# New hand-recorded operation lists, with later planned landings of the first loads, in a fused attention and channel-mix kernel

## The chip, the cores and the metric

The kernel runs on one core of one Trainium2 chip. A core has TensorE (PE, matrix products and transposes into PSUM), VectorE (DVE), ScalarE (ACT), GpSimd (POOL, used here to issue loads) and SyncE (SP, which issues other transfers). The metric is the device time of one execution in microseconds (us). The kernel before was run three times: 231.55, 230.36 and 232.74 us; its time is their median, 231.55 us.

## The reference

Attention over 8 batches, 8 heads, 576 rows of 64 numbers, with a causal window of 128 and a linear penalty for distance, and behind it a channel mix of the RWKV kind on its result:

```python
def _attn_ref(q, k, v):
    scores = np.matmul(q, k.transpose(0, 1, 3, 2)) / np.sqrt(D)
    rel = pos[:, None] - pos[None, :]
    slopes = 2.0 ** (-8.0 * (np.arange(H) + 1) / H)
    mask = (rel >= 0) & (rel < 128)
    scores = np.where(mask, scores - slopes * np.abs(rel), -1e9)
    attn = softmax(scores)
    return np.matmul(attn, v)

def _moe_ref(x, mu_k, mu_r, w_k, w_v, w_r):   # x: [8, 576, 512]
    x_prev = x shifted down by one row, zeros in front
    xk = mu_k * x + (1.0 - mu_k) * x_prev
    xr = mu_r * x + (1.0 - mu_r) * x_prev
    k = np.maximum(xk @ w_k, 0.0)             # 512 -> 1024
    v = k * k @ w_v                           # 1024 -> 512
    r = 1.0 / (1.0 + np.exp(-(xr @ w_r)))     # 512 -> 512
    return r * v
```

q, k, v, the weights and the output are float32 in memory; the products run in bf16.

## The kernel before, in words

**What one group does.** A batch's 8 heads are worked two at a time, in 4 groups (g = 0 to 3). For a group, q and k are brought into transposed form: by PE transposes and copies on ACT or DVE (L696, `copy_any`) in batches 0 to 4, and by transposing DMAs that SP issues (`flip`, L534; eight for a batch) in batches 5 to 7. Then `scores` (L698) multiplies k by q (L726) for the 576 x (128 + 128) band, ACT takes the exp from PSUM into the tile `at` (L740), and DVE multiplies it by a table of penalties (L753; batch 0 adds the penalty on PE instead). `attend` (L759) multiplies `at` by v, with a column of ones in v that gives the row sums (L781), and DVE takes the reciprocal and scales (L793) into `xu`. `xu` is transposed into `xt`: by PE and a copy, or, in batches 6 and 7, by a DMA that SP issues (`out_flip`, L899). `shift` (L863) takes the difference of neighbouring rows (L880) and two mixes, xk and xr (L887), all on DVE.

**The channel mix.** `channel_mix` (L968) is called for chunks of 256 to 512 rows of a pair of batches: eight products with w_k (L983), each followed by a relu on ACT (L990) and a square on DVE or ACT (L964), and then for each 128 rows one product with w_r (L1001), a tanh on ACT (L1008), two half products with w_v (L1017), a DVE step that joins them (L1022), and the store of 128 rows.

**Where the first data come from.** Batch 0 is worked in two parts, rows 0 to 255 and 256 to 575. The first part's q and k come in as float32 by four loads on SP's queue (q) and four on ACT's (k) (`first_load`, L544). All other loads are issued by POOL in program order: `LOADS = 'v2KtVkabRWwc'` gives the order for the beginning: two loads of v, the second part's q and k, the first half of w_k, the tail rows of q and k, two more loads of v and their tail (`tv_load`, L504), the second half of w_k, batch 1's q and k, its tail rows, w_r, the two halves of w_v, batch 1's v. After eight loads POOL waits for the load eight places back.

**What sets the order.** Every piece of work is a node of `Plan` (L89 to 238). A node has an engine, a duration, a latency, the nodes it depends on and the buffers it takes and gives back; `run` (L162) plays the whole kernel through in modelled time, on the host, and emits the instructions in that order. On PE, ACT and DVE the order is not chosen: `ORDER` (L22) lists, for each, the numbers of the operations in the order in which they stand on that engine, and an operation whose number may stand in either of two lists (a copy or a square) goes to the engine that lists it. Operations are numbered as they are added. POOL's order is the program's. SP's order is open: among the transfers that are ready in modelled time the plan takes the one of lowest priority, so that the modelled landing times and durations order SP's stores, flips and out flips. The model of a load is `dma` (L420): its issue, a shared queue named FAB that passes its kilobytes at `RATE`, and a latency of two parts, before and behind. None of these numbers reaches the chip, except through the order.

**Numbers that the prediction uses.** Operations 39 to 128 are the 90 fillers: products of a tile of zeros (L687, `emit_warm`), all depending on nothing but a memset. Operation 131 is the first transpose of q and k, the first real work on PE. Operations 15 to 18 are the DVE memsets of the two `tv` tiles (L480, `late`), for which the first `tv_load` waits. Operation 278 is the first product with w_r, in the place 141 of PE's list. Operations 1028 to 1060 are batch 7's groups 1 to 3; 1033, 1044 and 1055 are their attends. Operation 1090 is the w_r product of the third 128 rows of the chunk that begins at row 512 of the last pair.

Of the kernel before, what the change touches and what calls it, by code (L numbers as in the profile page):

```python
# [52 lines left out]
""".split()],  # L53
    "DVE": [int(x) for x in """
# [16 lines left out]
""".split()],  # L71
}

# [168 lines left out]
def kernel(  # L242
# [12 lines left out]
    nc = tc.nc  # L255
# [235 lines left out]
    def issue_t(nd):  # L491
        return 0.53 + 0.00034 * nd
# [835 lines left out]
```

## Time and profile before

| | |
|---|---|
| median of three runs | 231.55 us |
| the profiled execution: its own time | 230.37 us |
| the profiled execution: span of the core in the trace | 228.6 us |
| mean granted TensorE clock | 0.998 |
| transfers | 32.14 MB in 125629 packets |
| POOL's queue (q0) | 95728 packets, 16.26 MB |
| SP's and ACT's queue (q1) | 28128 packets, 14.89 MB |

The profile is of one execution, recorded on the chip. Times in it count from the start of the span; the execution's own time is 1.8 us longer. A line such as `L983 PE MATMUL uno<-xk,wk_sb ... x416` groups the instructions of line 983: what they write, what they read, how many there are. PEld is the weight load of TensorE, which runs beside the products. "SPq" and "POOLq" are the queues of transfers that SP and POOL issue. In rows with three numbers separated by strokes these are the least, the median and the greatest duration in ns. An arrow in square brackets names what ended an instruction's wait, after the microseconds of the wait. The window table gives for each stretch of the span each engine's busy time and number of instructions, the granted clock of TensorE, the share of the 16 DMA engines' time (a sum over queues, so it can pass 1) and the rate of transfer.

### The profile page before, as it was taken

What the parts mean: (1) busy time and instruction counts of PE and PEld (TensorE: products, weight loads), DVE (VectorE), ACT (ScalarE), POOL (GpSimd) and SP (SyncE); (2) the same over time, 40 slices, a digit from 0 to 9 for tenths busy, and PEclk for the clock granted to TensorE, in tenths of its full rate; (3) what the DMA queues carried; (4) which work ended last, traced back from release to release, by engine and by line L of the source; (5) the groups of instructions that cost most, each with busy time, mean ns of one, the idle gap of its engine ahead of it and who ended that gap; (6) DMA issues with size and microseconds to landing.
All of it is one profiled execution on the core that took longest, in us unless ns stands there. A gap on an engine that the chain in (4) does not pass through costs nothing.

```text
span 228.6 us, 6539 instructions
## 1 busy us (share of the span) xinstructions
PE 223.1 (98%) x2651; PEld 134.3 (59%) x2651; DVE 187.4 (82%) x417; ACT 160.9 (70%) x293; POOL 92.5 (40%) x118
## 2 busy tenths in 40 slices
PE   8999999999999999999999999999999999999994
PEld 8475856665666656545555755545665454456542
DVE  7585999899859999997869997999999986873423
ACT  3679999899998969997576757965758425326511
POOL 8676734889975980965004961600000000000000
PEclk9999999999999999999999999999999999999999
DMA  6999999999999999999965999995162134131123
GB/s 165 179 178 196 196 197 157 194 180 159 197 140 172 129 173 192 150 121 156 232 145 110 179 170 157 119 168 168 46 90 75 49 138 86 46 106 36 46 92 138
DMA packets 125629, 32.14 MB, mean 141 GB/s; under 512 B 112280, under 2 KB 121760, under 8 KB 125600
## 3 DMA queue, kind: packets, MB, share of 16 engines
q0 software_dynamic: 95728, 16.26, 102.5%
q1 hardware_dynamic: 28128, 14.89, 29.9%
q10 hardware_dynamic: 1744, 0.59, 1.1%
q8 instruction: 20, 0.33, 0.6%
q14 instruction: 9, 0.07, 0.1%
HBM read 33.56 MB, written 9.44 MB: 188 GB/s over the span
## 4 chain that ended last, share of the span: by engine, by line
PE 92%; ACT 3%; DMA 3%; SPq 1%; issue 0%; DVE 0%; DVEq 0%
PE uno L1017 28%; PE uno L983 27%; PE uno L1001 14%; PE duo L726 7%; PE duo L781 7%; DMA qx<-in_q_dram 3%; PE uno L837 2%; PE uno L687 2%; PE uno L1078 1%; PE uno L781 1%; PE duo L713 1%; ACT at L740 1%; SPq L550 1%; ACT qk L696 1%; ACT rl L990 1%; PE uno L1123 0%
## 5 line engine op out<-in xcount | busy, mean ns | idle before, releaser
L740 ACT ACTIVATE at<-duo 128x1024 bf16<-128x1024 f32 (+2 forms) x68 | 65.2, 986 | 9.6 <-PE duo L726 9.3
L983 PE MATMUL uno<-xk,wk_sb 128*128 128x256 bf16 (+2 forms) x416 | 71.4, 314 | 0.0
L1017 PE MATMUL uno<-wv_sb,kk 128*128 128x512 bf16 (+2 forms) x296 | 69.0, 374 | 0.0
L990 ACT ACTIVATE rl<-uno 128x256 bf16<-128x256 f32 (+2 forms) x104 | 46.8, 476 | 30.6 <-PE uno L983 25.0
L983 PEld LDWEIGHTS <-wk_sb 128*128 128x128 bf16 x416 | 38.5, 98 | 22.6 <-issue 0.5
L1017 PEld LDWEIGHTS <-kk 128*128 128x128 bf16 x296 | 27.3, 98 | 28.7 <-issue 0.2
L500 POOL DMA_DIRECT2D vs<-in_v_dram x32 | 28.5, 902 | 32.2 <-PE duo L781 29.9
L753 DVE TENSOR_TENSOR at<-at,mask 128x1024 bf16<-128x1024 bf16 x56 | 37.1, 684 | 4.2 <-ACT at L740 4.2
L1001 PE MATMUL uno<-wr_sb,xr 128*128 128x512 bf16 x144 | 36.5, 379 | 0.5 <-ACT rl L990 0.5
L964 DVE TENSOR_TENSOR kk<-rl 128x256 bf16<-128x256 bf16 (+2 forms) x90 | 28.5, 337 | 10.2 <-ACT rl L990 9.9
L1008 ACT ACTIVATE rs<-uno 128x512 bf16<-128x512 f32 x36 | 21.8, 607 | 16.3 <-PE uno L1001 15.2
L1022 DVE SCALAR_TENSOR_TENSOR ot<-rs,uno 128x512 f32<-128x512 bf16 (+2 forms) x37 | 24.4, 667 | 9.4 <-PE uno L1017 6.8
L887 DVE SCALAR_TENSOR_TENSOR xr<-dl,mu_sb,xt 128x576 bf16<-128x576 bf16 (+1 forms) x32 | 24.8, 774 | 0.0
L887 DVE SCALAR_TENSOR_TENSOR xk<-dl,mu_sb,xt 128x576 bf16<-128x576 bf16 (+1 forms) x32 | 24.5, 779 | 0.2
L781 PEld LDWEIGHTS <-at 128*128 128x128 bf16 x576 | 20.8, 98 | 4.2 <-DVE at L753 0.3
L793 DVE TENSOR_TENSOR xu<-duo,rc 128x640 bf16<-128x640 f32 x28 | 22.5, 814 | 0.3
L1001 PEld LDWEIGHTS <-xr 128*128 128x128 bf16 x144 | 13.3, 98 | 13.7 <-DMA wr_sb<-in_moe_w_r_dram 0.6
L531 POOL DMA_DIRECT2D cb<-in_k_dram x20 | 17.8, 910 | 5.6 <-DMA vs<-in_v_dram 4.8
L696 ACT COPY qk<-uno 128x512 bf16<-128x512 bf16 (+1 forms) x33 | 17.4, 588 | 1.8 <-PE uno L1126 1.0
L781 PE MATMUL duo<-vs,at 128*128 128x65 bf16 x448 | 18.6, 194 | 0.0
L531 POOL DMA_DIRECT2D cb<-in_q_dram x20 | 17.7, 924 | 1.0 <-PE duo L781 0.6
L696 ACT COPY xt<-uno 128x512 bf16<-128x512 bf16 (+3 forms) x28 | 15.4, 590 | 1.4 <-PE uno L837 0.7
(83 smaller groups left out, 202.2 us busy)
## 6 DMA issues: line engine op xcount, KB each, us to landing
out_dram<-ot SPq DMA_DIRECT2D x30, 256.0 KB, 4.6
vs<-in_v_dram POOLq DMA_DIRECT2D x32, 128.0 KB, 7.4
cb<-in_q_dram POOLq DMA_DIRECT2D x20, 128.0 KB, 6.7
cb<-in_k_dram POOLq DMA_DIRECT2D x20, 128.0 KB, 6.1
out_dram<-ot SPq DMA_DIRECT2D x10, 128.0 KB, 1.9
wk_sb<-in_moe_w_k_dram POOLq DMA_DIRECT2D x2, 512.0 KB, 8.2
cb<-in_q_dram POOLq DMA_DIRECT2D x4, 256.0 KB, 8.5
cb<-in_k_dram POOLq DMA_DIRECT2D x4, 256.0 KB, 8.8
```

The source lines that it names most:

```text
L500: return dma(POOL, 256, issue_t(1024), lambda e: nc.gpsimd.dma_start(out=vs_buf[h.idx][:, j, :, 0:D], in_=v[b, :, 128 * j:128 * j + 128].r ...
L531: return [dma(POOL, 256, issue_t(1024), lambda e, r=r: nc.gpsimd.dma_start(out=cb_buf[h.idx][:, i, r], in_=src[:, :, r]), [g], kind="q") f ...
L696: (nc.scalar.copy if e == ACT else nc.vector.tensor_copy)(out=out, in_=in_)
L740: lambda e, ah=ah, w=w, hp=hp: nc.scalar.activation(out=ah(), in_=two(hp)[:, :, 0:w], func=AF.Exp, scale=float(scale)), (), [hp])
L753: nc.vector.tensor_tensor(out=a, in0=a, in1=m, op=ALU.mult)
L781: nc.tensor.matmul(a[:, hl, t - t0], lhsT=at[:, lo:lo + 128], rhs=vs[:, u, 2 * g + hl, :] if u < NF else tvb[:, 2 * g + hl], start=(u == u ...
L887: lambda e: nc.vector.scalar_tensor_tensor(out=buf[hk.idx][:, g, e0 + c0:e0 + c1], in0=dls(), scalar=mu[:, g:g + 1], in1=xc(1), op0=ALU.mu ...
L964: nc.vector.tensor_tensor(out=out, in0=in_, in1=in_, op=ALU.mult)
L983: nc.tensor.matmul(one(hp)[:, 0:n], lhsT=wk_sb[:, po, 128 * fo:128 * fo + 128], rhs=xk_buf[hx.idx][:, po, c0:c1], start=(po == 0), stop=(p ...
L990: a = op(ACT, act_t(n), [s], pr, lambda e, hp=hp, hr=hr: nc.scalar.activation(out=rl_buf[hr.idx][:, 0:n], in_=one(hp)[:, 0:n], func=AF.Rel ...
L1001: nc.tensor.matmul(one(hp), lhsT=xr_buf[hx.idx][:, po, 128 * c:128 * c + 128], rhs=wr_sb[:, po], start=(po == 0), stop=(po == NPO - 1))
L1017: nc.tensor.matmul(one(hv)[:, a:b], lhsT=kk_buf[hk.idx][:, fo, o:o + 128], rhs=wv_sb[:, fo, a:b], start=(fo == 0), stop=(fo == NFO - 1))
```

## The change

The three lists in `ORDER` are replaced by others. They hold the same operations; 12 of them change the engine. PE's new list has 26 fillers instead of 31 ahead of operation 131. The four `tv` memsets (15 to 18) stand earlier in DVE's list, ahead of operation 149, batch 0's first reciprocal. Operation 1055 stands ahead of 1044 and 1033 instead of behind them, and 1090 at place 388 instead of 408 (counted from 1).

The plan gets three new constants. `FIRST` adds to the planned latency of the third and fourth of the first q and k loads on each queue, `VFIRST` to the planned kilobytes and latency of batch 0's v loads, `VLATE` 0.9 us to the planned latency of batch 1's. They change no transfer; through `run` they change the order of SP's queue, which is played anew with the new lists. Line numbers behind the constants move down by 3 to 8 lines, in `scores` and all that follows by 8.

The diff, with the inner lines of the lists cut:

```diff
 ORDER = {
     "PE": [int(x) for x in """
-42 76 47 65 59 73 39 58 48 50 71 68 63 74 75 41 43 55 46 61 40 66 51 52 45 56 57 67 70 53 69 131 60 44 49 72 144
-133 146 166 155 93 79 125 97 110 168 54 148 135 157 170 78 151 84 92 127 96 108 37 115 95 99 82 87 105 120 121
-86 106 173 159 64 83 124 118 62 123 81 184 119 128 122 111 138 100 116 90 112 102 85 101 77 98 117 103 162 89
-104 199 91 126 107 88 94 113 114 109 80 187 229 214 202 181 217 232 257 189 204 219 191 206 234 221 260 263 194
...
-904 885 1039 898 887 882 888 916 1028 924 921 892 922 883 926 893 927 1044 1033 976 988 973 1055 982 991 979 985
-1002 994 1007 997 1012 999 1009 1004 1000 1005 1010 1112 1121 1118 1061 1014 1067 1064 1076 1124 1103 1082 1109
-1115 1073 1100 1015 1070 1085 1079 1090 1092 1106 1093 1087 1097 1088 1126 1098 1095 1131 1127 1129 1132 1134
+75 65 44 77 46 42 61 50 41 40 43 59 45 63 53 66 48 57 56 39 72 49 47 76 68 69 131 71 51 67 58 74 144 133 146 52
+55 166 155 62 107 78 79 73 168 148 157 60 106 135 93 111 170 91 124 151 70 120 86 54 109 127 85 98 159 122 128
+101 117 138 87 112 82 84 173 115 108 96 105 121 37 116 81 64 119 123 184 83 114 162 118 100 92 103 102 89 113
+110 104 99 88 80 90 97 126 95 94 125 199 229 187 214 181 202 232 217 189 257 204 191 219 206 234 221 194 260 236
...
+910 901 924 1039 882 887 883 913 888 1028 885 976 973 921 1055 922 994 1044 991 979 926 892 927 1033 982 893 988
+1002 1007 985 997 1004 1012 999 1009 1000 1010 1090 1067 1100 1082 1005 1106 1061 1070 1076 1014 1079 1109 1085
+1115 1103 1064 1073 1015 1087 1124 1118 1088 1095 1097 1092 1121 1112 1098 1126 1093 1127 1131 1129 1132 1134
 1135
 """.split()],
     "ACT": [int(x) for x in """
-10 11 12 13 14 132 145 134 167 147 169 158 152 174 186 139 251 248 200 163 247 188 230 215 203 246 218 233 245
-190 258 205 220 250 259 235 244 261 249 195 264 225 267 255 210 357 270 240 356 256 268 273 325 276 361 359 279
-284 328 330 318 298 341 307 339 289 299 370 372 290 292 301 308 304 463 462 293 473 474 348 347 295 305 296 310
-505 504 313 311 302 378 379 476 478 493 494 509 393 507 399 402 394 496 408 498 396 411 405 406 390 387 421 388
...
-784 848 943 787 963 965 792 954 952 802 869 857 920 872 1020 881 1018 866 908 891 875 863 896 911 878 914 1053
-1051 860 902 886 1040 1042 899 905 917 1029 925 1031 977 989 974 992 983 980 986 1003 995 1008 1013 998 1113
-1062 1119 1122 1068 1077 1065 1125 1104 1083 1116 1074 1110 1071 1086 1080 1091 1101 1107 1096 1130 1137
+10 11 12 13 14 132 145 134 147 167 156 169 158 152 139 174 185 163 250 244 246 230 200 201 248 188 251 203 233
+218 190 247 205 249 220 258 245 235 195 261 210 264 225 267 270 240 357 255 356 256 276 273 325 361 359 279 367
+284 328 330 318 301 339 341 277 370 292 372 302 289 290 298 293 307 473 474 462 463 304 348 347 295 505 296 504
+313 310 305 311 379 308 378 478 476 494 493 507 408 509 399 393 496 498 411 387 402 388 396 390 570 571 421 572
...
+943 848 787 963 965 802 954 857 869 872 952 920 891 1018 1020 863 896 881 878 899 866 875 908 1053 905 860 1051
+902 925 1042 1040 917 914 911 886 977 1031 974 1029 995 980 992 983 1003 989 1008 986 998 1013 1091 1083 1101
+1068 1062 1071 1077 1107 1080 1110 1086 1104 1065 1074 1125 1116 1096 1119 1122 1113 1130 1137
 """.split()],
     "DVE": [int(x) for x in """
-0 2 6 4 7 5 1 34 29 3 28 26 9 27 32 25 30 129 130 31 142 143 15 17 36 8 33 22 35 19 18 156 20 149 136 150 137
-171 172 38 24 16 160 153 161 175 185 176 140 141 201 178 23 154 21 231 216 164 179 165 183 182 180 177 192 193
-207 208 222 223 262 237 238 265 226 196 227 197 228 323 198 326 241 211 243 212 242 368 213 367 336 337 277 271
-329 252 360 253 274 342 331 340 362 371 282 373 344 333 345 334 287 375 376 364 365 352 349 354 460 350 353 351
...
-1046 990 1056 978 1057 975 981 993 984 1058 1060 884 1047 996 1059 987 1048 1036 1037 1001 1038 1006 1011 1049
-1114 1063 1120 1069 1066 1078 1105 1084 1075 1111 1016 1072 1123 1081 1108 1102 1094 1117 1089 1099 1128 1133
-1136
+4 5 6 0 3 9 1 31 36 34 29 2 35 32 30 33 28 25 130 129 27 26 143 142 20 7 19 17 24 15 18 8 16 22 149 150 136 171
+137 172 160 153 161 140 38 175 176 186 178 231 180 21 216 215 182 183 23 141 164 154 165 179 177 192 193 207 208
+222 223 196 237 259 238 262 198 226 268 265 227 323 197 228 326 241 211 242 212 243 213 368 337 336 252 271 253
+329 274 360 331 340 362 342 371 282 287 344 373 345 333 334 375 299 376 364 365 349 352 350 460 353 354 351 383
...
+972 1046 981 1034 928 1035 996 993 894 1058 1059 1047 984 1048 990 1060 987 889 1036 1038 1037 1049 1001 1011
+1006 1102 1069 1084 1063 1078 1108 1111 1081 1105 1066 1072 1016 1075 1120 1089 1117 1123 1114 1094 1128 1099
+1133 1136
 """.split()],
 }
 
@@ -293,6 +293,9 @@
     NO = 5
     WAIT = 0.0
     START, BACK = 1.7, 0.25
+    FIRST = {'SP': (0.0, 0.0, 0.0, 0.7, 1.05, 1.05), 'ACT': (0.0, 0.0, 0.0, 0.85, 1.15, 1.15)}
+    VFIRST = ((0.0, 0.3), (0.0, 0.3), (60.0, 0.5), (60.0, 0.6), (40.0, 0.5))
+    VLATE = {1: 0.9}
     SKEW = {'v': 0.25, 'tv': 0.3, 'ts': 0.3}
     COST = {'first': 0.9, 'v': 1.2, 'q': 0.944, 'ts': 0.66, 'tv': 0.66, 'w': 0.88, 'run4': 1.0, 'run2': 1.03, 'flip': 1.0, 'mu': 1.0, 'x': 1.0}
     SS = ()
@@ -497,14 +500,16 @@
             out=dst()[:, i, h0:h1].rearrange("p h r d -> p h (r d)"), in_=hs), deps, kind='run%d' % r)
 
     def v_load(b, j, h, deps=()):
-        return dma(POOL, 256, issue_t(1024), lambda e: nc.gpsimd.dma_start(
+        return dma(POOL, 256 + (VFIRST[j][0] if b == 0 else 0.0), issue_t(1024), lambda e: nc.gpsimd.dma_start(
             out=vs_buf[h.idx][:, j, :, 0:D],
-            in_=v[b, :, 128 * j:128 * j + 128].rearrange("h p d -> p h d")), deps, kind="v")
+            in_=v[b, :, 128 * j:128 * j + 128].rearrange("h p d -> p h d")), deps, lat=(1.0, 0.9 + (VFIRST[j][1] if b == 0 else VLATE.get(b, 0.0))),
+            kind="v")
 
     def tv_load(b, h, deps=()):
-        return dma(POOL, 128 * TCOST, issue_t(512), lambda e: nc.gpsimd.dma_start(
+        return dma(POOL, 128 * TCOST + (VFIRST[4][0] if b == 0 else 0.0), issue_t(512), lambda e: nc.gpsimd.dma_start(
             out=tv_buf[h.idx][0:64, :, 0:D],
-            in_=v[b, :, SM:S].rearrange("h p d -> p h d")), deps, kind="tv")
+            in_=v[b, :, SM:S].rearrange("h p d -> p h d")), deps, lat=(1.0, 0.9 + (VFIRST[4][1] if b == 0 else VLATE.get(b, 0.0))),
+            kind="tv")
 
     def tail_load(b):
         h = Hold("ts")
@@ -541,13 +546,16 @@
         return dma(POOL, kb, 0.85, lambda e: nc.gpsimd.dma_start(
             out=dst, in_=src.rearrange("(i p) w -> p i w", p=128)), kind="w")
 
+    firsts = {SPE: [], ACT: []}
+
     def first_load(i, g, n):
         hs = (q, k)[i][0, 2 * g:2 * g + 2 * n]
         eng = KQ if i and g < 2 + KLAST else SPE
         qe = nc.scalar if eng == ACT else nc.sync
 
         def put(kb, dst, src):
-            return dma(eng, kb, 0.46, lambda e: qe.dma_start(out=dst, in_=src), lat=(1.54, 0.7), kind="first")
+            firsts[eng].append(kb)
+            return dma(eng, kb, 0.46, lambda e: qe.dma_start(out=dst, in_=src), lat=(1.54, 0.7 + FIRST[eng][len(firsts[eng])]), kind="first")
 
         if g not in FT:
             st = stage[:, g:g + n].rearrange("p g i w -> p (g i w)").rearrange(
```

42 rows, old and new, of the table ORDER are left out of this document.

## The prediction

> **What bounds the kernel now.** I read the page first (busy shares), then the table of windows, then the waits and the timeline around the one place where TensorE (PE) idles, then the tiles of the loads, then the chain of waits.
>
> ```profile
> PE 223.1 (98%) x2651; PEld 134.3 (59%) x2651; DVE 187.4 (82%) x417; ACT 160.9 (70%) x293; POOL 92.5 (40%) x118
> ```
> ```profile
> core 0: us, PE busy (x) PEld busy (x) DVE busy (x) ACT busy (x) POOL busy (x), PEclk, DMA share, GB/s
> 8.90:15.70 6.80, 6.80 (x136) 5.37 (x134) 5.21 (x21) 5.16 (x12) 3.63 (x5) 1.00 1.71 186
> 15.70:24.00 8.30, 8.13 (x149) 4.90 (x147) 5.36 (x18) 7.53 (x17) 5.61 (x9) 1.00 1.55 189
> 24.00:30.60 6.60, 6.10 (x132) 5.03 (x130) 5.79 (x17) 6.41 (x20) 3.88 (x5) 1.00 1.41 200
> 30.60:60.00 29.40, 29.39 (x492) 18.03 (x493) 28.08 (x54) 28.28 (x52) 22.22 (x27) 1.00 2.04 180
> 60.00:100.00 40.00, 40.00 (x585) 24.52 (x584) 36.48 (x74) 37.00 (x68) 28.80 (x35) 1.00 2.03 156
> 100.00:150.00 50.00, 50.00 (x551) 29.00 (x549) 43.42 (x90) 35.96 (x59) 20.77 (x25) 1.00 1.85 157
> 150.00:200.00 50.00, 50.00 (x410) 27.45 (x408) 45.40 (x91) 27.68 (x47) 0.00 (x0) 1.00 0.44 95
> 200.00:222.00 22.00, 22.00 (x128) 12.34 (x126) 9.93 (x24) 8.32 (x20) 0.00 (x0) 1.00 0.21 73
> ```
> The first column is the window, the second its length, the third PE's busy time. From 30.6 to 222 us PE is busy for 191.39 of 191.40 us at a granted clock of 1.00. The change keeps every operation, so after 30.6 us only small things can be won, and a new wait can be lost. What could be won lies before: PE idles 0.17 + 0.50 us between 15.7 and 30.6, and it runs fillers, matmuls on zeros.
>
> ```profile
> L687 PE MATMUL uno<-warm x90: 218/219/314, 1.0 to 15.6; 128*128 128x128 bf16 x90
> ```
> ```profile
> 29.51 0.56 PE L726 MATMUL duo<-qk 64*128 64x256 bf16 x8
> 29.94 0.19 PE L726 MATMUL duo<-tt 64*128 64x64 bf16 x2
> 30.61 1.04 PE L1001 MATMUL uno<-wr_sb,xr 128*128 128x512 bf16 x4 [0.48 <-ACT rl L990]
> ```
> ```profile
> L541 POOL DMA_DIRECT2D wr_sb<-in_moe_w_r_dram x1: 768/768/768, 19.4 to 19.4; - x1
>   PEld L1001: 0.6, 1
> DMA to landing us min/median/max: 11.2/11.2/11.2
> ```
> The last real work before 30.6 is the scores group at 29.51, over by about 30.1; then the first w_r product (L1001) starts at 30.61. Its load was issued at 19.4 and landed 11.2 us later, at 30.6: the weight w_r gates PE there, with some 0.5 us of idle time in front.
>
> **The change, part by part.** The POOL program holds the same transfers in the same order in both kernels. PE's list holds the same 423 operations. Its first 140 places hold the same set in both lists, and place 141 is the same w_r product. So whatever is reordered in front, PE meets the same gate with the same work done.
>
> *Is the gate moved?* One POOL wait should vanish:
>
> ```profile
> 12.71 0.69 POOL L505 DMA_DIRECT2D tv<-in_v_dram  x1 [2.94 <-DVE tv L480]
> 15.13 0.74 POOL L496 DMA_DIRECT2D cb<-in_k_dram  x1 [0.23 <-DMA wk_sb<-in_moe_w_k_dram]
> 18.73 0.68 POOL L521 DMA_DIRECT2D ts<-in_k_dram  x1 [0.65 <-DMA vs<-in_v_dram]
> ```
> ```profile
> 5.44 1.04 DVE L480 MEMSET tv<- 64x520 bf16 x2 [0.17 <-issue]
> 12.35 0.07 DVE L480 MEMSET tv<- 64x8 bf16 x1
> ```
> The tail load of v waits 2.94 us for the last of four memsets, which VectorE (DVE) does at 12.35. In the new DVE list all four stand ahead of the first reciprocal, beside the 1.04 us ones of 5.44, so the load can go at about 9.8. What it buys: this load and the two issues behind it go earlier; the one at 15.13 waits for a load to land (a DMA buffer eight loads back), and so does the one at 18.73, so w_r is still issued at 19.4. The windows show the transfers at 186 to 200 GB/s from 8.9 to 30.6, without a hole. I take 0 for the gate's move; its ends are 0 and, if the queue were not full, the idle time that the gate causes and the 0.17 before it, 0.67 us of gain, plus what the fillers' new places give (below).
> The Trainium skill, "DMA: Bandwidth & Descriptors", section "Anatomy of one DMA — SWDGE (gpsimd) path", gives about 2.0 us plus bytes over 436 GB/s for one such load; for w_r's 1 MB read that is an estimate of 4.4 us. By that, w_r would land at 23.8 and no gate would stand at 30.6. The trace has 11.2 us, so it queued; the measurement decides, but the page's rule is why I keep the faster rival below.
>
> *Fillers and first stage.* The 90 fillers stay 90. The first real product comes after 26 instead of 31; it waits for the first casts, which wait for the loads of q and k, so this costs nothing; without that cover 5 fillers are 5 x 0.11 = 0.5 us. The same masks, copies and exps run on ScalarE (ACT) in another order; ACT is busy 7.53 of 8.30 and 6.41 of 6.60 us here, and hands two squares to DVE. If this stage becomes faster the wait at the gate grows by as much; if it becomes up to 0.5 us slower the gate hides it. Price 0, bounds 0 and +0.5 (a stage 1 us slower).
>
> *ACT and DVE swaps.* Seven operations go from ACT to DVE and five the other way, all in the first 60 us: small copies and squares,
>
> ```profile
> L962 ACT ACTIVATE kk<-rl x6: 418/434/447, 28.8 to 44.2; 128x256 bf16<-128x256 bf16 x6
> L964 DVE TENSOR_TENSOR kk<-rl x4: 281/282/283, 26.2 to 37.5; 128x256 bf16<-128x256 bf16 x4
> ```
> at 0.43 us on ACT and 0.28 on DVE. Between 30.6 and 60 three engines are full at once (PE 29.39, ACT 28.28, DVE 28.08 of 29.40). There the new ACT list puts a q/k copy and a square in front of exps that the next score groups wait for: 0.43 to 0.6 us each. Lower end: a saved 0.1. Upper end: they fall on PE one for one and repeat, 2 us. I take 0.2, since ACT reaches 30.6 with less left to do.
>
> *Row switches.* A score group uses 64 rows, and the product behind it pays for the change:
>
> ```profile
> 105.12 0.65 PE uno L983 x4
> 105.77 0.55 PE duo L726 x12
> 106.32 0.97 PE uno L1017 x4
> ...
> 110.22 0.86 PE uno L1017 x4
> ```
> 0.97 against 0.86, 0.11 us. Counted in the lists, PE goes over to 64 rows 40 times before and 39 after: -0.1, with ends 0 and -0.2 (the entry costs as much).
>
> *SyncE's queue.* Its order is left to the plan, so new landing times reorder output stores and the transposing loads of the last three batches.
>
> ```profile
> L535 SPq DMA_TRANSPOSE qx<-cb x16: 1208/1228/2165, 110.5 to 149.6; - x16
> L726 PE MATMUL duo<-qx x72: 216/269/281, 111.7 to 159.6; 64*128 64x256 bf16 x54, 64*128 64x128 bf16 x18
> DMA to landing us min/median/max: 2.4/4.9/7.5
> ```
> The last of batch 7's is issued at 149.6 and its first scores run at 159.3 to 159.6, 7.5 us at worst to land: 2 us of cover. Three of these transposes now stand ahead of a store that held them for 3.7 us before. Price 0; if a store is late, 1.2 us for each transpose behind it.
>
> *The last attends.* Batch 7's groups were attended in the order 2, 1, 3 and are now in the order 3, 2, 1, with five w_k products moved ahead of the last; the first product on their result comes 12.6 us sooner in the list than before (it is now a w_r product).
>
> ```profile
> 185.13 0.62 PE L781 MATMUL duo<-vs,at 128*128 128x65 bf16 x15
> 188.27 0.62 PE L781 MATMUL duo<-vs,at 128*128 128x65 bf16 x15
> ```
> ```profile
> L902 SPq DMA_TRANSPOSE xt<-xu x3: 1199/1205/1221, 187.5 to 190.3; - x3
> DMA to landing us min/median/max: 2.6/2.6/2.6
> ```
> ```profile
> 193.41 0.45 DVE L880 TENSOR_TENSOR dl<-xt 128x576 bf16<-128x576 bf16 x1
> 193.90 0.82 DVE L887 SCALAR_TENSOR_TENSOR xr<-dl,mu_sb,xt 128x576 bf16<-128x576 bf16 x1
> ```
> Group 1, attended at 185.13, now has five more products of 0.86 and group 3's 0.55 in front and one of 0.86 less: 185.13 + 4.0 = 189.2. A short DVE step, one output step and the scaling bring its xu to about 191.7; transpose and landing to 194.5. DVE has twelve other steps in between (three mixes, two differences, five squares, two outputs), about 6 us, so it gets to this group at 197.7, and needs 0.48 + 0.73 + 0.73 + 0.82 = 2.8 us to the last xr: 200.4. The w_r product comes at 200.9. It is covered by 0.5 us on an engine busy 45.40 of 50 us. I take +0.1; lower end 0, upper end DVE's lag less 0.5.
>
> *The tail.* The closing four PE groups are the same. In front, the output row of the fifth chunk of the last pair moves from 217.4 to 222.8, so three rows instead of two are stored in the last 3 us.
>
> ```profile
> 222.54 0.69 DVE L1022 SCALAR_TENSOR_TENSOR ot<-rs,uno 128x512 f32<-128x512 bf16 x1 [2.53 <-ACT rs L1008]
> 223.43 0.69 DVE L1022 SCALAR_TENSOR_TENSOR ot<-rs,uno 128x512 f32<-128x512 bf16 x1 [0.20 <-PE uno L1017]
> 225.00 0.75 DVE L1022 SCALAR_TENSOR_TENSOR ot<-rs,uno 128x384 f32<-128x384 bf16 x2 [0.88 <-PE uno L1017]
> ```
> The steps themselves still fit (0.69 each between 222 and 225); one more row of 256 KB is in flight ahead of the last. +0.1, ends 0 and +0.4.
>
> Sum: 0 + 0 + 0.2 - 0.1 + 0 + 0.1 + 0.1 = +0.3 us. The profiled execution took 230.37 us (span 228.6 and 1.8 around it), so it would be 230.7. The median of the runs, 231.55, stands 1.2 above it; with +0.3 it is 231.8.
>
> **The rivals.** *A new wait in the last third (slower).* The w_r product of batch 7's last attended group waits for DVE. Against it stands the 0.5 us of cover worked out above, for it that DVE is 91% busy from 150 to 200 and that six mixes are crowded together. It decides once DVE is more than 0.5 us later there than I added up; 3 us late costs 2.5: 234.1.
> *The stretch of three full engines (slower, less).* Swapped copies hold exps, and PE waits 1 to 2 us between 30.6 and 60 where it waited 0.01: 233.0. For it: 96% on both ACT and DVE; against: as many operations left ACT as came.
> *The gate moves (faster).* If w_r lands earlier, PE saves the 0.67 us of idle time and up to 0.4 of fillers that now stand where it waits anyway: -1.1, with the +0.3 of the other terms 230.7. For it: the wait of 2.94 us goes; against: 186 to 200 GB/s throughout and the waits at 15.13 and 18.73. It can't give more, since 90 fillers stay in PE's order.
> That the change does nothing it was made for is my forecast itself: better landing times in the plan reorder the work in front of a gate that stays.
>
> **How the numbers follow.** Forecast 57%, 231.8 with its own range 230.8 to 232.8 (run spread of the median, the small terms); full engines 17%, 233.0; new wait 14%, 234.1; gate 12%, 230.7. About 1%, 2.3 us, is what a measurement of this kernel can tell from no change: faster is under 229.2, slower over 233.9. Faster: only a tenth of the forecast's and gate's cases by run spread, 0.07. Slower: the new wait and a little of the full engines, 0.16. Within: 0.77. Leaving out 2 in 10, the range is 230.0 to 233.8.
>
> **What would show it.** The tail load of v issued near 10 instead of 12.71, and the first w_r product still at 30.4 to 30.8 after a longer idle time: the gate right. PE idle under 0.5 us between 30.6 and 60: the swaps right. No wait of a w_r product near 201: the attends right. Wrong I am if the first w_r product starts a microsecond earlier, or if PE idles more than 1 us anywhere after 31.

## The result, and the profile after

Eight runs of each kernel: the changed kernel takes 233.42 us (232.74 to 234.07), the kernel before 230.95 us (230.13 to 233.97). The ratio is 1.0102, with a 95% interval of 1.0067 to 1.0137: the change costs 1%. The changed kernel's profiled execution has a span of 230.7 us, against 228.6 before.

The changed kernel's page, part 1, and its table of windows (the same stretches and columns as in the prediction; code lines now carry the changed kernel's numbers, 8 higher in most places):

```profile
PE 223.4 (97%) x2651; PEld 133.8 (58%) x2651; DVE 187.3 (81%) x419; ACT 160.3 (69%) x291; POOL 92.0 (40%) x118
```
```profile
8.90:15.70 6.80, 6.74 (x147) 5.20 (x143) 4.16 (x15) 4.70 (x11) 4.21 (x7) 1.00 1.75 184
15.70:24.00 8.30, 8.10 (x148) 4.84 (x135) 6.11 (x18) 7.61 (x18) 5.33 (x8) 1.00 1.52 190
24.00:30.60 6.60, 6.60 (x136) 5.22 (x133) 6.11 (x19) 6.41 (x17) 4.46 (x6) 1.00 1.39 200
30.60:60.00 29.40, 28.63 (x493) 17.84 (x492) 27.15 (x53) 27.75 (x51) 19.82 (x25) 1.00 1.94 172
60.00:100.00 40.00, 40.00 (x584) 24.52 (x581) 36.34 (x74) 35.67 (x66) 29.97 (x36) 1.00 2.14 160
100.00:150.00 50.00, 50.00 (x543) 28.98 (x542) 44.18 (x91) 36.41 (x60) 20.87 (x26) 1.00 1.73 158
150.00:200.00 50.00, 48.85 (x411) 26.86 (x409) 44.97 (x92) 27.43 (x47) 0.00 (x0) 1.00 0.46 88
200.00:222.00 22.00, 22.00 (x127) 12.31 (x126) 9.73 (x24) 9.18 (x21) 0.00 (x0) 1.00 0.19 67
```

PE's work is the same (223.4 against 223.1 us). Three rows of the third column differ from before by more than 0.1 us. Between 24.0 and 30.6 PE no longer idles (6.60 against 6.10): it gained 0.50. Between 30.6 and 60 it idles 0.77, where it idled 0.01. Between 150 and 200 it idles 1.15, where it did not idle at all. The first two about cancel; the third is the loss. The waits of the changed kernel from 160 to 180 us (who waited for what: us in all, times, longest) lead to it:

```profile
ACT rl L998 <- DVE kk L972: 5.6, 3, 3.1
DVE xu L801 <- DMA xt<-xu: 1.9, 1, 1.9
...
PE uno L991 <- ACT rl L998: 0.7, 1, 0.7
...
PE duo L734 <- DVE xu L801: 0.4, 1, 0.4
```

In the kernel before, the first of these is 1.7 us in all and the other three are not there. The one that the others hang on is the second: DVE's scaling into `xu` waited for a transfer that reads `xu`. The timeline of that place (start, duration, then in brackets the wait in front and what ended it):

```profile
168.10 0.22 DVE L795 RECIPROCAL rc<-duo 128x10 f32<-128x10 f32 x1 [0.31 <-PE duo L789]
...
170.27 0.82 DVE L801 TENSOR_TENSOR xu<-duo,rc 128x640 bf16<-128x640 f32 x1 [1.95 <-DMA xt<-xu]
...
170.38 0.39 PE L734 MATMUL duo<-qx 64*128 64x256 bf16 x4
...
171.15 0.34 PE L734 MATMUL duo<-qx 64*128 64x256 bf16 x4 [0.38 <-DVE xu L801]
...
171.45 0.76 ACT L998 ACTIVATE rl<-uno 128x384 bf16<-128x384 f32 x2 [3.14 <-DVE kk L972]
...
172.27 0.92 PE L991 MATMUL uno<-xk,wk_sb 128*128 128x256 bf16 x6 [0.72 <-ACT rl L998]
```

and the same two DVE steps in the kernel before, then PE's scores group and its next product:

```profile
168.09 0.22 DVE L787 RECIPROCAL rc<-duo 128x10 f32<-128x10 f32 x1
...
168.44 0.81 DVE L793 TENSOR_TENSOR xu<-duo,rc 128x640 bf16<-128x640 f32 x1
```
```profile
169.93 0.56 PE L726 MATMUL duo<-qx 64*128 64x256 bf16 x8
...
170.48 1.70 PE L983 MATMUL uno<-xk,wk_sb 128*128 128x256 bf16 x12
```

Both kernels take the reciprocal of batch 6's group 3 at 168.1. Before, the scaling (operation 969) follows at 168.44; after, DVE stands until 170.27. Behind it in DVE's list stand the squares that free the `rl` buffers ACT needs (3.14 us of wait), and ACT's relus free the PSUM tiles that PE needs; half of the scores group waits for the PSUM tile that the scaling itself reads (0.38). From the start of that group to the start of PE's next product it is 172.27 - 170.38 = 1.89 us. Before, it is 170.48 - 169.93 = 0.55.

What DVE waited for is the out flip of batch 6's group 1, issued at 165.2 and landed 5.0 us later, the longer of the first two of the train:

```profile
L910 SPq DMA_TRANSPOSE xt<-xu x2: 1203/1205/1207, 165.2 to 166.6; - x2
...
DMA to landing us min/median/max: 4.3/4.6/5.0
```

165.2 + 5.0 = 170.2, where the scaling starts. It writes into the buffer that this flip reads. There are four `xu` buffers, and number 3 lay free all the while: no group of batches 6 and 7 has it in the changed kernel. The choice is made on the host: `pick` (L131) takes the free buffer of the lowest number at the planned time. In the new plan the flip of group 1 is over when group 3 takes its buffer (with its reciprocal, 968); on the chip it landed 2.1 us after that reciprocal's start. What brings this about is the new order of DVE's list, where group 1's scaling (947) stands ahead of 1023 and 1024, and not the three new constants. Played on the host, the plan still gives group 3 that buffer with the constants at zero, and gives it number 3 with 947 put back behind 1024.

### The profile page after: what moved, and what is told of

It reads as the page before. It is cut to its first block, busy times and chain, and to the rows that moved or that the text cites. A ratio compares the mean times of both kernels' runs of the same rounds, so it can differ in the third digit from the quotient of the medians.

```text
span 230.7 us, 6560 instructions
## 1 busy us (share of the span) xinstructions
PE 223.4 (97%) x2651; PEld 133.8 (58%) x2651; DVE 187.3 (81%) x419; ACT 160.3 (69%) x291; POOL 92.0 (40%) x118
## 4 chain that ended last, share of the span: by engine, by line
PE 82%; DMA 9%; ACT 3%; DVE 3%; issue 1%; POOL 1%; POOLq 0%; DVEq 0%; ACTq 0%
PE uno L1025 26%; PE uno L991 25%; PE uno L1009 12%; PE duo L734 6%; PE duo L789 5%; DMA ts<-in_k_dram 4%; DMA vs<-in_v_dram 3%; PE uno L845 2%; DMA xt<-xu 2%; ACT at L748 2%; PE uno L695 1%; PE uno L789 1%; PE duo L721 1%; PE uno L1086 1%; DVE at L761 1%
## 5 line engine op out<-in xcount | busy, mean ns | idle before, releaser
L991 PE MATMUL uno<-xk,wk_sb 128*128 128x256 bf16 (+2 forms) x416 | 72.9, 314 | 0.8 <-ACT rl L998 0.7
L1025 PE MATMUL uno<-wv_sb,kk 128*128 128x512 bf16 (+2 forms) x296 | 70.1, 374 | 0.0
L998 ACT ACTIVATE rl<-uno 128x256 bf16<-128x256 f32 (+2 forms) x104 | 47.9, 479 | 31.3 <-PE uno L991 22.1
L972 DVE TENSOR_TENSOR kk<-rl 128x256 bf16<-128x256 bf16 (+2 forms) x94 | 30.0, 338 | 10.6 <-ACT rl L998 10.5
L801 DVE TENSOR_TENSOR xu<-duo,rc 128x640 bf16<-128x640 f32 x28 | 23.0, 821 | 2.5 <-DMA xt<-xu 1.9
L789 PEld LDWEIGHTS <-at 128*128 128x128 bf16 x576 | 21.6, 98 | 4.7 <-issue 0.5
L704 ACT COPY qk<-uno 128x512 bf16<-128x512 bf16 (+1 forms) x34 | 18.1, 583 | 4.6 <-PE uno L845 1.8
```

Of the source, the lines that this page charges most:

```text
L704: (nc.scalar.copy if e == ACT else nc.vector.tensor_copy)(out=out, in_=in_)
L789: nc.tensor.matmul(a[:, hl, t - t0], lhsT=at[:, lo:lo + 128], rhs=vs[:, u, 2 * g + hl, :] if u < NF else tvb[:, 2 * g + hl], start=(u == u ...
L972: nc.vector.tensor_tensor(out=out, in0=in_, in1=in_, op=ALU.mult)
L991: nc.tensor.matmul(one(hp)[:, 0:n], lhsT=wk_sb[:, po, 128 * fo:128 * fo + 128], rhs=xk_buf[hx.idx][:, po, c0:c1], start=(po == 0), stop=(p ...
L998: a = op(ACT, act_t(n), [s], pr, lambda e, hp=hp, hr=hr: nc.scalar.activation(out=rl_buf[hr.idx][:, 0:n], in_=one(hp)[:, 0:n], func=AF.Rel ...
L1025: nc.tensor.matmul(one(hv)[:, a:b], lhsT=kk_buf[hk.idx][:, fo, o:o + 128], rhs=wv_sb[:, fo, a:b], start=(fo == 0), stop=(fo == NFO - 1))
```

## The experiments

Each run stands beside runs of the kernel before on the same chip. e9 and e10 are one execution each, so only their traces are read, not their times.

| run | edit | us | before, us | ratio, 95% interval |
|---|---|---|---|---|
| e1_xu | changed kernel, xu buffer free longest | 231.73 | 231.28 | 1.0000 (0.9974 to 1.0026) |
| e2_new_head | new lists to 30 us, old behind | 231.99 | 231.28 | 1.0032 (1.0007 to 1.0057) |
| e3_old_head | old lists to 30 us, new behind | 233.60 | 231.28 | 1.0095 (1.0065 to 1.0125) |
| e4_less_stored | changed kernel, two stores cut | 232.65 | 231.28 | 1.0069 (1.0040 to 1.0097) |
| e5_swap | kernel before, two DVE steps exchanged | 231.39 | 231.34 | 0.9994 (0.9966 to 1.0022) |
| e6_swap_xu | e5 with the xu buffer free longest | 231.23 | 231.34 | 0.9999 (0.9977 to 1.0021) |
| e7_lone_flip | changed kernel, two flips left out | 231.65 | 231.34 | 1.0024 (0.9996 to 1.0051) |
| e8_new_head_xu_ot | e2, xu and ot free longest | 231.25 | 231.34 | 0.9990 (0.9961 to 1.0019) |
| e9_no_second | changed kernel, second flip left out | 232.55 | 230.91 | one execution |
| e10_no_third | changed kernel, third flip left out | 233.48 | 230.91 | one execution |
| e11_early_plan | kernel before, plan alone edited | 232.91 | 231.05 | 1.0075 (1.0037 to 1.0114) |

**Another buffer, nothing else.**

```diff
         free = self.free[h.cls]
+        if h.cls == "xu":
+            return min(free, key=lambda a: self.given.get(a, -1)) if free else None
         if h.cls not in self.pairs:
...
```

(`given` notes, for each buffer, when it was given back; the lines that fill it are left out.)

> The changed kernel, and of the four xu buffers the plan takes the one that has been free longest instead of the one of lowest number; no operation, no order of any queue and no duration of the plan changes. Theory (a buffer taken back too soon): in the changed kernel the scaling of batch 6's group 3 got the buffer that an out flip still read until 170.2, while another had been free since 155.6, and DVE stood 1.95 us. With the other buffer the scaling starts near 168.4, the scores group at 170.4 has no hole and PE loses 1.5 to 1.7 us less: 231.6 to 232.0 against 233.4. Rival (the order of SP's queue makes what follows late in any case): the differences and mixes behind wait for their own flips instead, and PE's hole moves a few microseconds on: 233.0 to 233.6.

The ratio fell from 1.0102 to 1.0000. (The 155.6 of the expectation is the landing of group 0's flip, whose buffer this run takes.) DVE's timeline in e1_xu:

```profile
167.87 0.22 DVE L801 RECIPROCAL rc<-duo 128x10 f32<-128x10 f32 x1 [0.31 <-PE duo L795]
168.12 0.82 DVE L807 TENSOR_TENSOR xu<-duo,rc 128x640 bf16<-128x640 f32 x1
```

No wait in front of the scaling, and PE is busy for 50.00 of 50.00 us between 150 and 200. All queues have the order of the changed kernel, so the rival, that SP's new order makes what follows late in any case, falls. The rule gives another buffer at 21 of the 36 takings of `xu`, but the changed kernel's trace names a wait of the scaling for a transfer at this place alone: within the interval, the cost of the change is this choice of a buffer.

**The lists mixed.** The operations that one plan starts before 30 us are listed in its order, the rest in the other's.

```diff
-    "PE": [...], "ACT": [...], "DVE": [...]
+    each list: [n for n in head[e] if n in early] + [n for n in rest[e] if n not in early]
```

> The three lists begin as in the changed kernel (all operations that its plan starts before 30 us) and go on as in the kernel before (the others, in its order). SP's order is that of the kernel before. Theory (the loads are a second gate): w_r lands near 29.4 and PE reaches its first w_r product at about 29.8 as in the changed kernel, 0.8 us ahead, but batch 2's q and k land at 44 to 46.6 however early PE is, so 0.4 to 0.8 us are given back between 42 and 49: 230.3 to 231.0, against 230.95 of the kernel before. Rival (the lead is kept, and only the new order of the stretch behind lost it): 230.0 to 230.3.

231.99: the lead is not kept, but the time came out worse than either theory had it. The profile of e2_new_head shows why. It has a hole of its own, of the same making in another kind of buffer:

```profile
111.31 0.69 DVE L1022 SCALAR_TENSOR_TENSOR ot<-rs,uno 128x512 f32<-128x512 bf16 x1 [1.30 <-DMA out_dram<-ot]
...
113.04 0.56 PE L726 MATMUL duo<-qx 64*128 64x256 bf16 x8 [0.76 <-DVE xu L793]
```

DVE waited 1.30 us for a store that still read the `ot` buffer the plan had given again, and PE's next scores stood 0.76 us. (e8 tests this.)

> The three lists begin as in the kernel before (all operations that its plan starts before 30 us) and go on as in the changed kernel. The scaling of batch 6's group 3 still gets the buffer of an out flip in flight. Theory: w_r lands near 30.6, the first w_r product starts there, and PE then waits less for batch 2's loads, since it comes to them 0.8 us later; the hole at 170 stays at 1.4 to 1.7 us: 233.2 to 233.7. Rival (the lead at the first gate is worth its 0.8 us to the end): 234.1 or more.

233.60, as the theory had it: with the old lists in front the loss is still there, so it is made behind 30 us. Its profile has the hole at 170 (PE 48.92 of 50.00 us from 150 to 200), and another of 1.10 us at 51.7, which neither parent has and whose cause the trace does not name. So the number was met partly by luck: the first hole is smaller than the theory's 1.4 to 1.7, and the second was not in it.

**The stores beside batch 2's loads.**

```diff
+                            hi = lo + 16 if row < 256 else hi
                             nc.sync.dma_start(
                                 out=of[row:row + 128, lo:hi], in_=ot_buf[ho.idx][:, lo:hi])
```

> The changed kernel, with the stores of the first 256 output rows cut to 16 of 512 columns, so those rows of the output are not whole. Theory (the two stores, issued at 40.7 and 41.3 in the changed kernel and about a microsecond later before, take the transfers that batch 2's q and k need): the second k load of batch 2 lands at 45.6 or earlier instead of 46.6, PE's holes between 42 and 49 shrink from about 0.7 to 0.2 us, and the time falls to 232.7 to 233.0. Rival (POOL's queue passes them at its own pace): they land within 0.3 us of where they did, 233.2 to 233.6.

Batch 2's second q and k loads (tile `cb`) landed 8.1 to 8.5 us after their issue. In the changed kernel one of the two takes 9.3:

```profile
L499 POOL DMA_DIRECT2D cb<-in_k_dram x1: 740/740/740, 37.5 to 37.5; - x1
...
DMA to landing us min/median/max: 8.1/8.3/8.5
```
```profile
L499 POOL DMA_DIRECT2D cb<-in_k_dram x1: 742/742/742, 37.3 to 37.3; - x1
...
DMA to landing us min/median/max: 8.0/8.7/9.3
```

The slow one is the second k load: it landed at 46.6, and in e4 at 45.6, as the theory had it. The other traces point the same way. In the six where both stores go at 40.5 to 42.2 (the changed kernel, e1, e3, e7, e9, e10) that load takes 9.1 to 10.7 us; in the six where the second store goes at 44.6 or later (the kernel before, e2, e5, e6, e8, e11) it takes 8.2 to 8.8. So the stores, issued early, delay this load by about a microsecond. What that is worth stays open; the time, 232.65, lies just under the theory's range: PE was busy 9.62 of 10 us between 40 and 50 against 9.37, but it also came there later (its first w_r product ran at 30.58), and the intervals of the two ratios overlap.

**The smallest trigger in the kernel before.**

```diff
-... 946 1023 1024 947 ...
+... 946 947 1023 1024 ...
```

> The kernel before with one edit: in DVE's list the scaling 947 (batch 6, group 1) stands ahead of 1023 and 1024 (reciprocal and scaling of batch 7's group 0) instead of behind. By the plan SP then issues the out flip of 947 ahead of that of 1024, frees buffer 0 of xu earlier in its modelled time and gives it to 968 (batch 6, group 3), where the kernel before gives buffer 3. Theory (a buffer taken back too soon): DVE waits 1.5 to 2 us at 168.5 for the flip of 947, the scores group 1050 has a hole of over 1 us, and the time rises by 1.3 to 1.8 us: 232.3 to 233.1 against 231.3 of the kernel before. Rival (it takes the changed kernel's whole order of that stretch): two neighbours of 0.8 us exchanged cost at most 0.2 us, 231.1 to 231.5.

The expectation failed: 0.9994. The plan did give the buffer of the flip in flight, but that flip landed in time. The rows of e5_swap, the flip issued at 165.9 by tile, and DVE:

```profile
L902 SPq DMA_TRANSPOSE xt<-xu x1: 1206/1206/1206, 165.9 to 165.9; - x1
...
DMA to landing us min/median/max: 2.6/2.6/2.6
```
```profile
168.73 0.22 DVE L787 RECIPROCAL rc<-duo 128x10 f32<-128x10 f32 x1
...
169.09 0.82 DVE L793 TENSOR_TENSOR xu<-duo,rc 128x640 bf16<-128x640 f32 x1
```

165.9 + 2.6 = 168.5, before the scaling could start in any case. So a buffer given again too soon costs only when the flip is late.

> The kernel before with the same exchange in DVE's list, and the xu buffer that has been free longest. Theory: back to the kernel before, 231.1 to 231.5, no wait of the scaling at 168.5. Rival (the early flip itself costs): as with the exchange alone, 232.3 to 233.1.

It came out at 231.23, level with e5's 231.39, so it does not tell the theories apart.

**Why the flip lands late.**

```diff
+            if (b, g) in ((7, 0), (6, 2)):
+                return
             nc.sync.dma_start_transpose(
```

> The changed kernel without the two out flips that SP issues right behind the flip of 947 (batch 7's group 0 and batch 6's group 2), so two blocks of xt keep what was in them. It asks why the flip of 947 lands 5 us after its issue where the last three of the kernel take 2.6. Theory (transposes issued back to back land together, at the end of their train): alone it lands 2.6 us after its issue, near 167.9, the buffer is free when the scaling of group 3 wants it, and the hole at 170 is gone: 231.6 to 232.1. Rival (5 us is its own time there): the flip still lands near 170.2 and the hole stays at over 1 us: 233.1 to 233.7.

The flip landed 3.2 us after its issue (not 2.6), DVE waited 0.2 us, PE had no hole (50.00 of 50.00 us from 150 to 200), and the time was 231.65. Then each of the two alone was left out:

> The changed kernel without the out flip of batch 7's group 0, the second of the train (a block of xt keeps what was in it). The flip of batch 6's group 2 then follows the first one by some 2.5 us instead of 1.4. If the flip directly behind holds back the landing of the first, it lands 2.6 us after its issue and the scaling of batch 6's group 3 starts at 168.2 to 168.8. If it is the third flip (whose issue took 2.4 us in the changed kernel instead of 1.2), the first still lands near 170 or when the third has been issued, and the scaling waits over 1 us.

> The changed kernel without the out flip of batch 6's group 2, the third of the train (a block of xt keeps what was in it). If the flip directly behind holds back the landing of the first, it still lands 4.5 to 5 us after its issue and the scaling of batch 6's group 3 waits over 1 us. If it is the third, the first lands 2.6 us after its issue and there is no wait.

The first flip in e9_no_second (second left out), and in e10_no_third (third left out):

```profile
L912 SPq DMA_TRANSPOSE xt<-xu x1: 1206/1206/1206, 166.6 to 166.6; - x1
...
  DVE xu L801: 0.2, 1
...
DMA to landing us min/median/max: 3.2/3.2/3.2
```
```profile
L912 SPq DMA_TRANSPOSE xt<-xu x1: 1207/1207/1207, 166.0 to 166.0; - x1
...
  DVE xu L801: 2.0, 1
...
DMA to landing us min/median/max: 5.0/5.0/5.0
```

So in this train the first lands late only with a flip directly behind it; the third makes no difference. But a flip directly behind is not enough. In e5 and e6 the first flip also had one and landed after 2.6 us, and so did the kernel before's flips at 187.5 to 190.3, which go 1.3 to 1.5 us apart. The packets in the traces show what else ran: a load of instructions, one packet of 16 KB on queue q8.

```profile
q8 instruction: 1, 0.02, 1.1%
```

(This is the changed kernel from 164 to 173 us; from 186 to 193 the kernel before has no such row.) In the changed kernel the load ran from 167.58 to 169.18. A flip's landing is counted by 16 semaphore increments. All packets of the first flip had started by 167.5, and one of its increments came at 168.28, but then packets of the flip behind stood until 170.0, and the other 15 increments came from 170.03 on. In all eleven traces in which a flip follows directly, packets of that flip stand until 0.8 to 0.9 us after the instruction load has ended, and in nine of them at least one increment of the first flip, and so its landing, comes only then: 4.2 to 5.1 us after the issue. In e5 and e6 all 16 increments came before the packets stood. In e7 and e9, with the load but no flip directly behind, it is 3.2. No run takes the load away, so its part is read from the traces and not shown by an experiment; and it is not the only thing that makes a flip late: batch 6's first out flip, issued at 150.4 in the changed kernel soon after the last transposing loads, landed after 5.1 us with no such load.

**The same choice forced on the kernel before.** An out flip's planned latency is shortened; its lists and the order of every queue stay as they were.

```diff
-        return [fab(SPE, FLIP * NJ / 4, n, FLAT, [hx], True)]
+        return [fab(SPE, FLIP * NJ / 4, n, (0.1, FLAT[1]), [hx], True)]
```

> The kernel before, with its own lists; in the plan alone an out flip is taken to land 0.3 us earlier. No queue's order changes; of the xu buffers one choice does: 968 (batch 6, group 3) now gets buffer 1, which the flip of 1024 (batch 7, group 0) reads, instead of buffer 3. (Two rl and eight PSUM buffers get other numbers too.) Theory (a buffer taken back too soon): the flip of 1024 lands near 170.1, the scaling of group 3, which started at 168.44, waits for it 1.5 to 1.8 us, and PE's scores group behind it has a hole of about a microsecond: 232.2 to 233.1 against 231.3. Rival (the kernel before has room for such a wait, and the changed lists behind 165 us are needed to feel it): DVE waits, PE does not, 231.1 to 231.6.

1.0075, slower beyond its interval: a loss of the same kind as the changed kernel's, made in the kernel before by one number of the plan. e11_early_plan at the same place:

```profile
170.12 0.82 DVE L793 TENSOR_TENSOR xu<-duo,rc 128x640 bf16<-128x640 f32 x1 [1.53 <-DMA xt<-xu]
...
171.00 0.34 PE L726 MATMUL duo<-qx 64*128 64x256 bf16 x4 [0.61 <-DVE xu L793]
...
171.74 1.47 PE L983 MATMUL uno<-xk,wk_sb 128*128 128x256 bf16 x10 [0.34 <-ACT rl L990]
```

The same chain: DVE 1.53, the scores 0.61, the next products 0.34. The eight PSUM and two `rl` buffers that also changed their numbers show no wait of their own there. The trace is of one of the faster executions (231.67 us, of 231.27 to 234.34), and PE idles 0.95 us in it between 150 and 200; the rest of the 0.75% it does not show.

**The same choice, in ot.** e2 with the buffer choice of e1 for `xu` and `ot`.

> The lists of the run with the new head (changed kernel's lists up to 30 us, those of before behind), and for xu and ot, the two kinds of buffers that transfers read, the one that has been free longest. In the run with the new head DVE waited 1.30 us at 111.3 for a store to leave its ot buffer, and PE's scores at 113.0 had a hole of 0.76. Theory (the same choice of the lowest number): that wait goes and the time falls by 0.7 to 0.9 us, from 232.0 to 231.1 to 231.3, level with the kernel before. Rival (all five ot buffers are busy there, so none can be taken): the wait stays, 231.8 to 232.1.

231.25, a ratio of 0.9990 where e2 had 1.0032: as the theory has it, though the two intervals overlap. PE is busy for 50.00 of 50.00 us between 100 and 150, where e2 had 49.24. No version here beats the kernel before beyond its interval; e1 and e8 are level with it.

## Why the prediction was right, and where it was wrong

The range held the time and the sign was right, but the forecast was +0.3 us and the change costs 2.47; the likeliest case was not what happened. By its own sign the prediction was wrong: it named PE idling more than 1 us anywhere after 31, and at 170 PE stood 0.38 + 0.72. That the range reached to 233.8 it owes to rivals whose waits did not come, so that it held the time is luck.

*The gate.* The tail load of v was issued at 10.29 (9.8 was forecast), and w_r at 19.4 as before, as forecast. But the gate did move: w_r landed 10.0 us later instead of 11.2, at 29.4.

```profile
29.83 1.04 PE L1009 MATMUL uno<-wr_sb,xr 128*128 128x512 bf16 x4
```

The first w_r product started 0.78 us earlier, with no wait in front. Part of it is scatter: in the profiles of both kernels and of all runs but e8 (whose profiled execution, 234.64 us, lies 3.4 above its median) w_r lands between 29.4 and 30.9. In these the first product starts at 29.8 to 30.6 with the new head (seven) and at 30.3 to 31.4 with the old (five); the means lie 0.6 us apart, so the step "0 for the gate's move" was some 0.6 us too high. The gain did not last, because of what the prediction did not price: batch 2's q and k come no sooner for a PE that does, and the second k load lands at 46.6 instead of 45.5, behind two stores that go earlier (e4). Between 40 and 50 PE is busy 9.37 us in the changed kernel, and was 10.00 before:

```profile
40.00:50.00 10.00, 9.37 (x236) 6.79 (x236) 8.26 (x18) 8.99 (x22) 6.56 (x9) 1.00 1.79 185
```
```profile
40.00:50.00 10.00, 10.00 (x246) 6.80 (x245) 9.24 (x19) 9.32 (x23) 8.20 (x11) 1.00 1.86 192
```

The 10.00 is not fixed: in e5 and e6, with the old lists there, it is 9.67 and 9.70, so up to half of the difference may be scatter. The rival of the moved gate had the cause half right, and left out the next load behind it. That these loads took the gain back is read from PE's waits there; no run shows it by itself.

*The three full engines.* PE idled 0.77 us between 30.6 and 60, over the 0.5 that the prediction set as its mark. Of the waits of PE that the trace names between 40 and 50, both end on batch 2's loads (`cb` and `ts`, 0.2 us each), none on a swapped copy. The price of 0.2 for the swaps can't be told from nothing.

*SyncE's queue.* This is the step that failed. It was priced at 0, with a late store as the only cost; the runs show the buffer's wait in its place, 1.95 us of DVE and about 1.1 of PE, and 1.0102 against 1.0000 in time. The prediction looked at the transposing loads and the stores, and at how long transfers take to land; it did not ask which buffer each planned landing gives back, and to whom. The plan's times do more than order a queue: they choose buffers. The diff does not show it, since no buffer's size or count changes. So the sentence ahead of the prediction, that none of the plan's numbers reaches the chip except through the order, does not hold: e11 left the order of every queue as it was and cost 0.75%.

*The last attends.* The sum put the last xr at 200.4 and the w_r product on it at 200.9. In the changed kernel, some 2 us behind by then, they are at

```profile
201.32 0.81 DVE L895 SCALAR_TENSOR_TENSOR xr<-dl,mu_sb,xt 128x576 bf16<-128x576 bf16 x1
```
```profile
203.06 1.03 PE L1009 MATMUL uno<-wr_sb,xr 128*128 128x512 bf16 x4
```

so 202.1 and 203.1: covered, by 0.9 instead of 0.5, and without a wait. The rival "a new wait in the last third" came nearest, 234.1 against 233.42, with PE stopped by a late DVE; but its place was 170 and not 201, and DVE was late by a buffer and not by its load. It was the right kind of number for the wrong reason.

*The tail.* From ACT's last store to the end of the span it is 230.7 - 228.06 = 2.64 us, and before 228.6 - 225.78 = 2.82: no cost, where 0.1 was taken.

```profile
228.06 0.36 ACTq L1049 DMA_DIRECT2D out_dram<-ot  x1
```
```profile
225.78 0.37 ACTq L1041 DMA_DIRECT2D out_dram<-ot  x1
```

*The sum.* With the one wait taken away (e1) the change costs 231.73 - 231.28 = 0.45 us by medians and nothing by the ratio, 1.0000 with 0.26% on either side. The +0.3 that was forecast for all its small terms lies in that. The rest of the 2.47 us between the medians, some 2 us, goes with the missed term, since it goes away with it in e1. The trace shows 1.89 - 0.55 = 1.34 of it at the scores group itself; where the remaining 0.7 lies is not shown, and it is no more than the scatter of single executions.

## What to carry to other kernels

Where a modelled time decides which of several buffers is used next, compare the modelled landing with the traced one for every transfer that reads a buffer; a reordering that looks free can hand out a buffer still being read. Taking the buffer that has been free longest, instead of the one of lowest number, cost nothing here and removed the wait. And a gain at one load was not kept here, where the next load did not come earlier too.

## What the runs showed of the hardware

A transposing DMA of 128 x 640 bf16 from SBUF to SBUF lands 2.6 us after its issue at the end of the kernel, with or without another directly behind it. At 165 to 170 us, where an instruction load of 16 KB runs, it is 3.2 with the next one left out and 4.2 to 5.1 with another issued 0.1 to 0.2 us after its own issue ended, but 2.6 in e5 and e6; a third behind makes no difference (e10, 5.0). The Trainium skill, "DMA: Bandwidth & Descriptors", section "Queues, rings and completion order", has the semaphore's increment land after every earlier write of the same DMA engine, and names no later transfer that it would wait for. That is an order and gives no time, and these runs do not decide whether it accounts for the late increments: in the changed kernel 503 of the 640 data packets of the flip behind had started, from 167.75 to 168.55, before 15 of the first flip's 16 increments came.
